# New order constants, TensorE squares for the weights and half chunks in a fused block-sparse attention and MoE kernel

## The chip, the cores and the metric

The kernel runs on one core of a Trainium2 chip. The metric is the device time of one execution in microseconds (us). An execution counts as changed when it differs from the time before by more than 2%.

## The reference

Block-sparse attention over 4 batches, 8 heads, 768 positions and 64 dimensions, followed by a feed-forward layer over the resulting 3072 tokens of width 512. Inputs and outputs are float32, except that the two weight matrices come as 8-byte floats and the sampled blocks as 8-byte integers.

```python
scores = (q @ k.transpose(0, 1, 3, 2)) / sqrt(64)          # 768 x 768 per head
mask = |block_i - block_j| <= 1                            # blocks of 32 positions
mask |= block_i in (0, 23) or block_j in (0, 23)           # first and last block: always
mask |= block_j in sampled_blocks[block_i]                 # 3 random blocks for each row block
attn = softmax(where(mask, scores, -1e9))
x = (attn @ v) as 3072 tokens x 512
h = x @ w_in                                               # w_in 512 x 2048
g = max(h, 0) + alpha * min(h, 0)                          # alpha: one per column of h
return g @ w_out                                           # w_out 2048 x 512
```

## The kernel before

**Precision.** Matmuls run in float16, and float32 accuracy comes from splits: a matrix is scaled by a power of two and split into a high part "hi" (the float16 nearest to it) and a low part "lo" (what is left). A product is then three products: hi by hi, hi by lo, lo by hi. The power of two comes from the sum of the matrix's squares.

**Attention.** A unit is one batch, one tile of 128 queries and one quad of heads: 48 units, of which 8 (the last query tile of each batch) are dense and 40 sparse. A sparse unit has scores against the always present and the neighbouring blocks (tile `sp`, from `kt` with `qt` and `qs`), scores against the random blocks (`sp` from `kr`, which GpSimd gathers with block numbers held in registers), a softmax (VectorE writes `e` and the maximum `nm`, ScalarE the exponential), a split of the probabilities (`ph`), their transpose by DMA (`pt`), and products with the values: random ones (`vr`, gathered by SyncE's DMAs with block numbers in registers), boundary ones (`vb`) and the rest (`v`), all into `av`. Two quads make a tile of x, which is split (`xn`) and transposed by DMA.

**Feed-forward.** 12 chunks of 256 tokens. A chunk has 8 "up" groups and 8 "down" groups. An up group is 24 matmuls 128x256 into the one tile `h` that TensorE has for it (L1174); VectorE then makes `g` of it (L1183 twice, L1184), ScalarE `gh` (L1188), GpSimd `gl` (L1192), and a down group is 12 matmuls 128x512 into the chunk's two `o` tiles (L1209).

**Weights.** 16 pieces of each matrix arrive as raw 8-byte words (512 KB a piece) on the queues of SyncE and ScalarE. VectorE rebuilds float32 from them in three steps (L1033, L1040, L1045), ScalarE sums the squares (L390), and the split follows. w_in has one scale for each pair of pieces. w_out has a single scale: the squares of all 16 pieces are summed (`otot`, a matmul `tot<-ident,otot`, L565) before any piece is split, and so before the first down group. w_in's raw words lie in the space that w_out takes later; w_out's raw words lie in spare buffers of `x` and `vr`.

**Order.** A planner (class Plan) is given every operation with a priority, the engines that may take it, an estimate of its cost and the buffers it needs, and writes out one list for each engine while the program is built. At run time each engine works strictly through its list, and so does each engine's DMA queue: an instruction that waits holds up everything behind it on its engine, DMA issues included. Changing a priority therefore changes what stands behind what.

**Start.** GpSimd loads the sampled blocks by nine DMAs (L276, L281, L286) and clamps them (`sidx`, L315), VectorE packs them in pairs (`spack`), and GpSimd and SyncE load them into registers (L323).

Of the kernel before, what the change touches and what calls it, by code (L numbers as in the profile page):

```python
# [8 lines left out]
F32 = mybir.dt.float32  # L9
# [17 lines left out]
MOE_LAG = 14.222  # L27
MOE_BOOST = 7.439
V_WI = 2.0
W_WI = 0.799  # L30
V_WO = 4.06
W_WO = 1.152
WI_LO = "pe"
PL_W = 30.0
PL_V = -46.0
P_V = -3.693
P_K0, P_K1 = -10.0, 3.746
KB0, KB1, KL0, KL1 = -5.461, -8.133, -22.947, -14.0
VB0, VB1, VL0, VL1 = -4.453, -6.0, -20.0, -9.725
GK, GV = (6, 3), (5, 3)  # L40
P_Q, PL_Q = 10.31, 12.632
A_UP = 0.511
X_UP = 0.863
LD = 3
LAG = 0
# [4 lines left out]
K_PE = 2  # L50
Q_PE = 1
P_PE = 0
# [16 lines left out]
class Plan:  # L69
# [5 lines left out]
    LAT = {"PE": 0.2, "DVE": 0.2, "ACT": 0.2, "POOL": 0.15}  # L75
# [26 lines left out]
    def run(self):  # L102
# [46 lines left out]
        while left:  # L149
            progress = True  # L150
            while progress:
# [4 lines left out]
                for o in ready:  # L156
                    if not self.fits(o.alloc):
                        continue
                    best = min(o.alts, key=lambda e: max(idle[e] - now, hold(o, e)) + load[e] + cost(o, e))
# [57 lines left out]
def attn_moe(ctx: ExitStack, tc: tile.TileContext, q, k, v, sampled, w_in, w_out, alpha, out):  # L217
# [53 lines left out]
    smp = sampled.bitcast(I32).rearrange("a (r w) -> a r w", w=2)  # L271
    srow = cpool.tile([P, NT, NR, 2], I32, name="srow")
    for g in range(NG4):
        rows = [4 * t + 1 + g for t in range(TS)]
        part = srow[g * BLK : (g + 1) * BLK]
        nc.gpsimd.dma_start(  # L276
            part[:, :TS].rearrange("p t r w -> p t (r w)"),
            smp[rows[0] : rows[-1] + 1 : 4].rearrange("t r w -> t (r w)").partition_broadcast(BLK),
        )
        last = (4 * TS + 1 + g) % NBLK  # L280
        nc.gpsimd.dma_start(  # L281
            part[:, TS].rearrange("p r w -> p (r w)"),
            smp[last].rearrange("r w -> (r w)").partition_broadcast(BLK),
        )
    rawp = cpool.tile([P, NBLK * NR * 2], I32, name="rawp")
    nc.gpsimd.dma_start(rawp[BLK : BLK + 1], smp.rearrange("a r w -> (a r w)").unsqueeze(0))  # L286
    sraw = rawp[BLK : BLK + 1].rearrange("p (a r w) -> p a r w", r=NR, w=2)
    al_r = rawp[:NF, :P].bitcast(F32)
    nc.gpsimd.dma_start(al_r, alpha.rearrange("(f p) -> f p", p=P))
# [5 lines left out]
    spare = wi[:, 0, : 2 * P].bitcast(U8)  # L295
# [4 lines left out]
    for x in phs:  # L300
# [12 lines left out]
    ident16 = cpool.tile([P, P], F16, name="ident16")  # L313
    nident = cpool.tile([P, P], F16, name="nident")
    nc.gpsimd.tensor_scalar(sidx, sraw[:, :, :, 0], 0, NBLK - 1, ALU.max, ALU.min)  # L315
    pairs = sidx.rearrange("p a r -> p (a r)")[:, NR : NR + TS * NG4 * NR].rearrange("p (n w) -> p n w", w=2)
    nc.vector.scalar_tensor_tensor(
        spack, pairs[:, :, 1], 16, pairs[:, :, 0], ALU.logical_shift_left, ALU.bitwise_or
    )
    idx = {}  # L320
    for name, eng in (("g", nc.gpsimd), ("s", nc.sync)):
        regs = [eng.alloc_register(name=f"{name}{i}") for i in range(TS * NG4 * NR // 2)]
        eng.load(regs, spack)  # L323
        idx[eng] = []
        for r in regs:
            v = eng.snap(r)
            idx[eng] += [
                nc.s_assert_within(x, 0, NBLK - 1, skip_runtime_bounds_check_because="clamped to this range before the load")
                for x in (v & 0xFFFF, v >> 16)
            ]  # L330
    nc.gpsimd.tensor_copy(sf, srow[:, :, :, 0])
# [16 lines left out]
    nc.gpsimd.tensor_copy(ident16, ident)  # L348
# [60 lines left out]
    LQ3 = {"ACT": 1.3, "SP": 1.0}  # L409
    MAX4 = {"DVE": (0.57, 0), "ACT": 0.89, "POOL": 1.05}  # L410
# [463 lines left out]
    def gather(u, gate):  # L874
        b, t, c = units[u]
        n = 4 * u
        T["krb", u] = plan.buf("kr")
        T["okr", u] = plan.op(n - 4, {"POOL": 3.2}, lambda: emit_kr(u), o_kt[b, c] + chain("kr"), [T["krb", u]], [kbuf[b, c]])
        tail["kr"] = T["okr", u]
        if c == 0:  # L880
            T["vrb", b, t] = plan.buf("vr")
            T["ovr", b, t] = plan.op(n - 3, {"SP": 6.3}, lambda: emit_vr(b, t), o_scr[b] + gate + chain("vr"), [T["vrb", b, t]], dma=2.0)
# [120 lines left out]
    isum = cpool.tile([P, NF], F32, name="isum")  # L1003
    osum = cpool.tile([P, NF], F32, name="osum")
# [7 lines left out]
    def emit_load_w(e, name, f, h):  # L1012
        if name == "wi":
            r = wo.rearrange("p a b -> p (a b)").bitcast(I32)[:, (f % 8) * 1024 : (f % 8 + 1) * 1024]
            load(e, r.rearrange("p (c j) -> p c j", j=W2), wi_src[:, f, :, :])
            T["raw", name, f, h] = r
            return
        t = wt(h.pool, [P, 1024], I32, "raw")
        load(e, t, wo_src[:, f, :])
        T["raw", name, f, 0] = t  # L1020
# [26 lines left out]
    def emit_w_sq(name, f):  # L1047
        w, acc = (wi, isum) if name == "wi" else (wo, osum)
        squares(w[:, f + 1, :], acc[:, f : f + 1])

    def emit_g_norm(g):
        T["itot", g] = ps_h.tile([P, W2], F32, tag="h", name="itot")
        for i in range(2):
            nc.tensor.matmul(T["itot", g][:, 0:1], ones, isum[:, 2 * g + i : 2 * g + i + 1], start=(i == 0), stop=(i == 1))
# [25 lines left out]

    def wparts(name, f):
        w, w16 = (wi, wi16) if name == "wi" else (wo, wo16)
        s = ssc[:, f // 2 : f // 2 + 1] if name == "wi" else s_wo
        return w[:, f + 1, :], w16[:, f, 512:1024], w16[:, f + 1, 0:512], s
# [9 lines left out]
    def emit_sid(g):  # L1094
        T["sid", g] = wt("sid", [P, P], F32)
        nc.gpsimd.tensor_scalar(T["sid", g], ident, ssc[:, g : g + 1], 1.0, ALU.mult, ALU.mult)

    def emit_w_lo_pe(f):
        w, hi, lo, s = wparts("wi", f)
        T["d", f] = ps_o.tile([P, 512], F32, tag="o", name="d")  # L1100
        nc.tensor.matmul(T["d", f], T["sid", f // 2], w, start=True, stop=False)  # L1101
        nc.tensor.matmul(T["d", f], nident, hi, start=False, stop=True)

    def emit_w_lo_copy(f):
        w, hi, lo, s = wparts("wi", f)
        nc.scalar.copy(lo, T["d", f])

    def win(hl, f, c):
        o = 512 if hl == 0 else 0
        return wi16[:, f + hl, o + c * P : o + (c + 1) * P]  # L1110

    def wout(hl, f):
        o = 512 if hl == 0 else 0
        return wo16[:, f + hl, o : o + 512]
# [5 lines left out]
    o_wi, o_wo, o_n3 = {}, {}, {}  # L1120
    n3wi, sqs, gs = {}, {}, []
    for f in range(NF):
        p = V_WI + W_WI * f
        o = plan.op(p - PL_W, LQ, lambda e, f=f: emit_load_w(e, "wi", f, 0), [n3wi[f - 8]] if f >= 8 else [], [plan.buf("ld")], dma=1.6)
        o = plan.op(p, {"DVE": (0.4, 0)}, lambda f=f: emit_n1("wi", f, 0), [o])
        o = plan.op(p, {"ACT": 1.27, "DVE": (0.65, 0)}, lambda e, f=f: emit_n2(e, "wi", f, 0), [o])
        n3wi[f] = plan.op(p, {"DVE": (0.65, 0)}, lambda f=f: emit_n3("wi", f, 0), [o])
        sqs[f] = plan.op(p, {"ACT": 0.8}, lambda f=f: emit_w_sq("wi", f), [n3wi[f]])
        if f % 2 == 1:
            hb = plan.buf("h")  # L1130
            o = plan.op(p - 2, {"PE": 0.8}, lambda g=f // 2: emit_g_norm(g), [sqs[f - 1], sqs[f]], [hb])
            gs.append(plan.op(p - 2, {"DVE": 0.27}, lambda g=f // 2: emit_g_scale(g), [o], [], [hb]))
            prev = o_wi.get(f - 2)
            sb = plan.buf("sid")
            o_sid = plan.op(p, {"POOL": 0.5}, lambda g=f // 2: emit_sid(g), [gs[-1], prev], [sb])
            for x in (f - 1, f):
                o = plan.op(p + 0.1, {"ACT": 0.63, "DVE": (0.36, 0), "POOL": 0.82}, lambda e, x=x: emit_w_hi(e, "wi", x), [gs[-1], prev])
                if WI_LO == "pe":
                    db = plan.buf("o")
                    o = plan.op(p - 2, {"PE": 1.2}, lambda x=x: emit_w_lo_pe(x), [o, o_sid], [db], [sb])  # L1140
                    prev = o_wi[x] = plan.op(p, {"ACT": 0.5}, lambda x=x: emit_w_lo_copy(x), [o], [], [db])
                else:
# [202 lines left out]
```

## Time and profile before

| | |
|---|---|
| median of 3 runs | 851.91 us (842.58, 851.91, 854.73) |
| profiled execution | 850.29 us, its span 848.5 us |
| mean granted TensorE clock | 0.935 |
| busy TensorE / VectorE / ScalarE / GpSimd | 724.1 / 610.0 / 381.9 / 353.2 us |
| DMA | 137.95 MB, mean 163 GB/s |

The span starts with the first instruction and ends with the last; the profiled execution is 1.8 us longer than its span. In the views shown further down, a row of the timeline has the start and duration in us, engine, line, operation, tiles, and in brackets the idle time before it and what ended it. A row of groups has a count, then busy us and mean ns of one, then the idle time before. A row of the table by stage has the stage, its length, then busy us (and instructions) of TensorE matmuls, TensorE weight loads, VectorE, ScalarE and GpSimd, then the granted clock, the DMA engines' busy share and GB/s. A share of the DMA engines can read a little over 1.

### The profile page before, as it was taken

What the parts mean: (1) busy time and instruction counts of PE and PEld (TensorE: products, weight loads), DVE (VectorE), ACT (ScalarE), POOL (GpSimd) and SP (SyncE); (2) the same over time, 40 slices, a digit from 0 to 9 for tenths busy, and PEclk for the clock granted to TensorE, in tenths of its full rate; (3) what the DMA queues carried; (4) which work ended last, traced back from release to release, by engine and by line L of the source; (5) the groups of instructions that cost most, each with busy time, mean ns of one, the idle gap of its engine ahead of it and who ended that gap; (6) DMA issues with size and microseconds to landing.
All of it is one profiled execution on the core that took longest, in us unless ns stands there. A gap on an engine that the chain in (4) does not pass through costs nothing.

```text
span 848.5 us, 24338 instructions
## 1 busy us (share of the span) xinstructions
PE 724.1 (85%) x9163; PEld 502.7 (59%) x9163; DVE 610.0 (72%) x1444; ACT 381.9 (45%) x846; POOL 353.2 (42%) x670
## 2 busy tenths in 40 slices
PE   0644834779998799799999989899999999999997
PEld 0522523556676477566776666576767676667664
DVE  1796679889998576669987747787886677776332
ACT  2654544647544342546644415544444444443111
POOL 4582326534528332735374625321545343121221
PEclk9956865799999899999999999999999999999999
DMA  7799599999999798998977989999776989464000
GB/s 146 212 268 240 143 179 226 210 197 172 188 171 174 187 175 147 195 182 159 208 153 158 193 158 184 181 186 171 136 169 170 178 161 187 76 127 76 23 16 25
DMA packets 359094, 137.95 MB, mean 163 GB/s; under 512 B 326320, under 2 KB 340672, under 8 KB 358976
## 3 DMA queue, kind: packets, MB, share of 16 engines
q1 hardware_dynamic: 304416, 107.92, 67.1%
q10 hardware_dynamic: 54240, 28.45, 14.2%
q8 instruction: 72, 1.18, 0.6%
q14 instruction: 46, 0.38, 0.2%
q0 software_dynamic: 320, 0.03, 0.1%
HBM read 56.65 MB, written 12.58 MB: 82 GB/s over the span
## 4 chain that ended last, share of the span: by engine, by line
PE 56%; DVE 15%; DMA 12%; issue 7%; POOL 4%; ACT 3%; SPq 1%; POOLq 1%; ACTq 1%; DVEq 0%
PE o L1209 21%; PE h L1174 21%; PE sp L638 6%; PE av L638 5%; DMA pt<-ph 3%; DVE ph L402 3%; DVE g L1183 2%; DMA raw<-in_moe_w_out_dram 2%; DMA vr<-scr 1%; PE d L1101 1%; POOL kr L633 1%; POOL gl L1192 1%; DMA qf<-in_q_dram 1%; DVE e L722 1%; DVE wo L402 1%
## 5 line engine op out<-in xcount | busy, mean ns | idle before, releaser
L1174 PE MATMUL h<-x,wi 128*128 128x256 f16 x2304 | 270.8, 275 | 14.9 <-DVE g L1184 13.6
L1192 POOL TENSOR_TENSOR gl<-g,gh 128x512 f16<-128x512 f32 x96 | 120.8, 1259 | 318.4 <-ACT gh L1188 289.9
L1174 PEld LDWEIGHTS <-wi 128*128 128x128 f16 x2304 | 223.7, 99 | 49.8 <-issue 16.6
L1209 PE MATMUL o<-wo,gh 128*128 128x512 f16 x768 | 233.5, 386 | 6.1 <-ACT gh L1188 6.1
L633 POOL COPY kr<-kt 128x128 f16 x480 | 162.1, 388 | 61.0 <-PE sp L638 56.0
L1188 ACT CAST gh<-g 128x512 f16<-128x512 f32 x96 | 59.1, 615 | 216.1 <-DVE g L1184 168.1
L1209 PE MATMUL o<-wo,gl 128*128 128x512 f16 x384 | 147.8, 385 | 6.2 <-POOL gl L1192 6.2
L1183 DVE TENSOR_SCALAR g<-h,am 128x256 f32<-128x256 f32 x192 | 83.7, 477 | 89.2 <-PE h L1174 78.2
L402 DVE SCALAR_TENSOR_TENSOR ph<-e,ph 128x704 f16<-128x704 f32 (+1 forms) x110 | 109.6, 1004 | 14.2 <-ACT ph L394 13.8
L1209 PEld LDWEIGHTS <-gh 128*128 128x128 f16 x768 | 71.4, 99 | 80.1 <-ACT gh L1188 7.1
L729 ACT ACTIVATE e<-e,nm 128x352 f32<-128x352 f32 x160 | 92.6, 579 | 48.6 <-DVE nm L722 28.0
L722 DVE CUSTOM_DVE_ANT_0 e<-sp,bias,cs 128x352 f32<-128x352 f32 x160 | 87.7, 576 | 10.4 <-PE sp L638 10.4
L638 PE MATMUL sp<-kt,qt 128*128 128x192 f16 (+2 forms) x384 | 66.2, 246 | 25.8 <-DVE nm L722 24.6
L638 PEld LDWEIGHTS <-pt 96*32 96x32 f16 (+1 forms) x3456 | 74.0, 99 | 21.7 <-issue 8.5
L638 PEld LDWEIGHTS <-qt 128*32 128x32 f16 (+1 forms) x1024 | 47.6, 101 | 51.2 <-issue 29.3
L1184 DVE SCALAR_TENSOR_TENSOR g<-h,gsc,g 128x512 f32<-128x512 f32 x96 | 72.1, 751 | 3.4
L1209 PEld LDWEIGHTS <-gl 128*128 128x128 f16 x384 | 38.1, 99 | 57.0 <-POOL gl L1192 11.0
L638 PE MATMUL sp<-kt,qs 128*128 128x192 f16 (+2 forms) x384 | 66.2, 246 | 0.5 <-DVE vtot L570 0.5
L394 ACT ACTIVATE ph<-e 128x704 f16<-128x704 f32 (+1 forms) x68 | 54.4, 803 | 3.1 <-DVE g L1183 1.8
L638 PE MATMUL av<-v,pt 128*128 128x64 f16 x1056 | 55.2, 195 | 0.0
L638 PEld LDWEIGHTS <-qs 128*32 128x32 f16 (+1 forms) x1024 | 43.6, 102 | 5.2 <-issue 2.3
L747 ACT ACTIVATE e<-e,nm 128x768 f32<-128x768 f32 x32 | 29.8, 933 | 37.1 <-DVE nm L743 29.5
(153 smaller groups left out, 781.6 us busy)
## 6 DMA issues: line engine op xcount, KB each, us to landing
vr<-scr SPq DMA_DIRECT2D x240, 64.0 KB, 2.6
wo<-in_moe_w_in_dram SPq DMA_DIRECT2D x12, 512.0 KB, 4.7
raw<-in_moe_w_out_dram SPq DMA_DIRECT2D x12, 512.0 KB, 4.8
qs<-qt SPq DMA_DIRECT2D x46, 128.0 KB, 3.5
out_dram<-ob ACTq DMA_DIRECT2D x20, 256.0 KB, 4.0
scr<-v SPq DMA_DIRECT2D x10, 384.0 KB, 3.2
kf<-in_k_dram ACTq DMA_DIRECT2D x9, 384.0 KB, 5.4
vf<-in_v_dram ACTq DMA_DIRECT2D x24, 128.0 KB, 5.7
```

The source lines that it names most:

```text
L394: nc.scalar.activation(dst, src, AF.Copy, scale=scale)
L402: nc.vector.scalar_tensor_tensor(dst, src, scale, hi, ALU.mult, ALU.subtract)
L633: nc.gpsimd.tensor_copy(kr[:, :, g, r * BLK : (r + 1) * BLK], kt[:, :, bass.ds(i * BLK, BLK)])
L638: nc.tensor.matmul(dst, lhs, rhs, start=start, stop=False, skip_group_check=True)
L722: nc.vector.tensor_tensor_reduce(T["e", u, h // 2][:, h % 2, :CS], T["sp", u, h][:, :CS], bias[:, t], scale=T["cs", b, t][:, c : c + 1], s ...
L729: nc.scalar.activation(e, e, AF.Exp, bias=T["nm", u, h], scale=-1.0, accum_out=su_of(u, h))
L1174: nc.tensor.matmul(ph[:, i, :], win(w, f, ct), x[:, l, ct, :], start=(m == 0), stop=(m == len(terms) - 1))
L1183: nc.vector.tensor_scalar(g[:, i, :], ph[:, i, :], 0.0, am1[:, f : f + 1], ALU.min, ALU.mult)
L1184: nc.vector.scalar_tensor_tensor(g, ph, gsc[:, j : j + 1], g, ALU.mult, ALU.add)
L1188: nc.scalar.copy(T["gh", c, j], T["g", c, j])
L1192: nc.gpsimd.tensor_tensor(T["gl", c, j], T["g", c, j], T["gh", c, j], ALU.subtract)
L1209: nc.tensor.matmul(T["o", c][t], g[:, i, t * P : (t + 1) * P], wout(w, f), start=(f == 0 and m == 0), stop=(f == NF - 1 and m == 2),)
```

## The change

Eleven edits, in one step.

1. The priorities and planner constants are new numbers. A penalty (PEN0, PEN1) is added to VectorE's cost wherever the planner chooses between engines, so more splits go to GpSimd and ScalarE. LD (weight loads under way at once) goes from 3 to 2.
2. Weight loads are issued by ScalarE alone (W_ACT), `vb` loads by SyncE alone.
3. The sampled blocks come by one DMA to all partitions, and the register loads become operations of the plan.
4. The weights' squares are summed on TensorE: a pair of pieces is 8 matmuls 128x128 of a block with itself (bf16, the high half of each float32; tile `wsq`), and VectorE takes the diagonal of each. 16 pairs in all.
5. ScalarE's other squares (q, k, v) are written to `rawp` instead of a part of `wi`.
6. The chain of splits of each matrix, in which a piece waited for the piece before it, is cut in two halves that run beside each other.
7. Any of three engines may make `sid` (the scaled identity by which TensorE makes w_in's low part).
8. w_out is taken in reverse; 9 of its 16 pieces wait in w_out's own space (SLOT), 7 in the buffers of `x` and `vr`.
9. `emit_act`: two instructions 128x256 become one of 128x512 with a broadcast factor.
10. The first two chunks run in halves of 128 tokens: 4 up groups of 48 matmuls 128x128 and 4 down groups of 12 matmuls 128x512 for each half.
11. Q_PE goes from 1 to 3 and P_PE from 0 to 2: the first query tiles and the first units' probabilities are transposed on TensorE instead of by DMA.

```diff
-MOE_LAG = 14.222
+MOE_LAG = 13.556
...
-V_WO = 4.06
-W_WO = 1.152
+V_WO = -2.805
+W_WO = 1.818
...
-LD = 3
+LD = 2
+PEN0, PEN1 = 0.3, 0.72
+W_ACT = 1
+HALF = 2
+Q_PE = 3
+P_PE = 2
...
-    smp = sampled.bitcast(I32).rearrange("a (r w) -> a r w", w=2)
...
+    smp = sampled.bitcast(I32).rearrange("a (r w) -> (a r w)", w=2)
+    rawp = cpool.tile([P, 3 * W2 // 4], I32, name="rawp")
+    nc.gpsimd.dma_start(rawp[:, : NBLK * NR * 2], smp.partition_broadcast(P))
...
+    o_regs = {
+        "POOL": plan.op(-11, {"POOL": 3.5}, lambda: emit_regs(nc.gpsimd, "g"), [o_pack]),
+        "SP": plan.op(P_REG, {"SP": 3.5}, lambda: emit_regs(nc.sync, "s"), [o_pack]),
+    }
...
-            o_vb[b, t] = plan.op(n - 3, LQ3, lambda e: emit_vb(e, b, t), o_scr[b] + gate, [vbb[b, t]], dma=0.6)
+            o_vb[b, t] = plan.op(n - 3, {"SP": 1.0}, lambda e: emit_vb(e, b, t), o_scr[b] + gate, [vbb[b, t]], dma=0.6)
...
+    SLOT = {15: 0, 14: 1, 12: 2, 11: 3, 9: 0, 8: 1, 6: 2, 5: 1, 4: 0}
...
-    def emit_w_sq(name, f):
-        w, acc = (wi, isum) if name == "wi" else (wo, osum)
-        squares(w[:, f + 1, :], acc[:, f : f + 1])
+    def emit_w_sq(name, fs, tag):
+        w = wi if name == "wi" else wo
+        t = T["wsq", name, fs[0] // 2] = (ps_h if tag == "h" else ps_o).tile([P, 512], F32, tag=tag, name="wsq")
+        blocks = [
+            w[:, f + 1, c * P : (c + 1) * P].bitcast(BF16).rearrange("p (e w) -> p e w", w=2)[:, :, 1]
+            for f in fs for c in range(NC)
+        ]
+        for i, x in enumerate(blocks):
+            nc.tensor.matmul(t[:, :P], x, x, start=(i == 0), stop=(i == len(blocks) - 1))
...
-        for i in range(2):
-            f = 2 * j + i
-            nc.vector.tensor_scalar(g[:, i, :], ph[:, i, :], 0.0, am1[:, f : f + 1], ALU.min, ALU.mult)
-        nc.vector.scalar_tensor_tensor(g, ph, gsc[:, j : j + 1], g, ALU.mult, ALU.add)
+        a2 = am1[:, n * j : n * j + n].unsqueeze(2).broadcast_to([P, n, w])
+        nc.vector.scalar_tensor_tensor(g, ph, 0.0, a2, ALU.min, ALU.mult)
+        for i in range(0, n, 2):
+            f = (n * j + i) // 2
+            nc.vector.scalar_tensor_tensor(g[:, i : i + 2], ph[:, i : i + 2], gsc[:, f : f + 1], g[:, i : i + 2], ALU.mult, ALU.add)
...
+    for half in range(2):
+        prev = None
+        for f in range(half * NF // 2, (half + 1) * NF // 2):
+            prev, o_wo[f] = split("wo", f, p + 0.1 * f, [o_swo], prev, f < W_PE, o_sid, sb)
...
+    def whole(c):
+        if c >= HALF:
+            return moe(c)
+        for half in range(2):
+            moe(c, half)
```

The lists of the engines show what moved. At the start of SyncE's list, before (`kf`, `qf`, `vf` are raw keys, queries and values of the first batch; `wo<-in_moe_w_in_dram` is a raw piece of w_in):

```order
L323 TENSOR_LOAD spack
L326 ISA x3
L418 DMA kf<-in_k_dram 128x12x64
L418 DMA qf<-in_q_dram 128x8x64
L418 DMA kf<-in_k_dram 128x12x64
L418 DMA vf<-in_v_dram 128x4x64 x3
L418 DMA wo<-in_moe_w_in_dram 128x4x256 x2
```

and in the changed kernel:

```order
L425 DMA kf<-in_k_dram 128x12x64
L425 DMA qf<-in_q_dram 128x8x64
L425 DMA kf<-in_k_dram 128x12x64
L425 DMA vf<-in_v_dram 128x4x64 x3
L368 TENSOR_LOAD spack
L371 ISA x3
L425 DMA vf<-in_v_dram 128x4x64 x6
```

The register load now stands behind the first keys, queries and values, and the raw pieces of w_in have left this list.

The last two raw pieces of w_out, before, on SyncE's list (`x<-xn`, `pt<-ph` and `qt<-qn` are transposes by DMA; `kf` and `qf` here belong to the second batch):

```order
L793 DMA_TRANSPOSE x<-xn 128x8x128
L772 DMA_TRANSPOSE pt<-ph_102 128x12x128
L418 DMA raw<-in_moe_w_out_dram 128x1024
L465 DMA_TRANSPOSE qt<-qn 128x8x128
L418 DMA kf<-in_k_dram 128x12x64 x2
L418 DMA qf<-in_q_dram 96x8x64
L418 DMA qf<-in_q_dram 32x8x64
L418 DMA raw<-in_moe_w_out_dram 128x1024
L772 DMA_TRANSPOSE pt<-ph_103 128x12x128
```

and the last one in the changed kernel, on ScalarE's list (`e,su<-e,nm` is the exponential of a pair of heads, `gh<-g` the feed-forward's high part):

```order
L1249 CAST gh<-g 128x512
L736 ACTIVATE e,su<-e,nm 128x352
L400 ACTIVATE ph_95<-e 128x2x352
L425 DMA raw<-in_moe_w_out_dram 128x1024
L1249 CAST gh<-g 128x512
L736 ACTIVATE e,su<-e,nm 128x352 x2
L789 CAST xn<-xf 128x512
L1049 ACTIVATE raw<-raw 128x512
L425 DMA kf<-in_k_dram 128x12x64 x2
```

The last piece has changed queues, and the second batch's keys now follow it instead of standing ahead of it; ahead of it stand softmax and feed-forward instructions of ScalarE.

On TensorE the matmul `tot<-ident,otot` has, before, ahead of it the scores of units 1 to 8, the random scores of units 1 to 8 and five up groups; in the changed kernel the scores and random scores of units 1 to 7 and the work of four up groups (four half groups of 48 matmuls). The first down group comes behind it in both, and by the scores of unit 11 both lists have issued 13 up and 12 down groups. From there on the two lists stay level to the end.

More of the change, by code (lines that the diff above doesn't have):

```diff
@@ L158, in run @@
                         continue
-                    best = min(o.alts, key=lambda e: max(idle[e] - now, hold(o, e)) + load[e] + cost(o, e))
+                    best = min(o.alts, key=lambda e: max(idle[e] - now, hold(o, e)) + load[e] + cost(o, e) + (PEN0 if now < 150 else PEN1) * (e == "DVE"))
                     if hold(o, best) > 1e-9:
@@ L269, in attn_moe @@
     v_nat = [v[b].rearrange("h (t p) d -> p t h d", p=P) for b in range(B)]
-    smp = sampled.bitcast(I32).rearrange("a (r w) -> a r w", w=2)
[L272 to L289, printed above, removed]
+    smp = sampled.bitcast(I32).rearrange("a (r w) -> (a r w)", w=2)
+    rawp = cpool.tile([P, 3 * W2 // 4], I32, name="rawp")
+    nc.gpsimd.dma_start(rawp[:, : NBLK * NR * 2], smp.partition_broadcast(P))
+    sraw = rawp[:, : NBLK * NR * 2].rearrange("p (a r w) -> p a r w", r=NR, w=2)
+    ident16 = cpool.tile([P, P], F16, name="ident16")
+    nc.gpsimd.tensor_copy(ident16, ident)
     wi = cpool.tile([P, NF + 1, 512], F32, name="wi")
@@ L1122, in attn_moe @@
+    prev = None
     for f in range(NF):
         p = V_WI + W_WI * f
[L1124 to L1128, printed above, removed]
+        slots[f % 8].append(weights("wi", f, p, p - PL_W, None, slots[f % 8][-1:], []))
@@ new lines, in attn_moe @@
+    o_gsc = plan.op(V_WI + W_WI * NF - 2, {"DVE": 0.5}, emit_gsc, gs + [o_al])
+    osq, done = [], {}
+    for n, f in enumerate(reversed(range(NF))):
+        p = V_WO + W_WO * n
+        s, rb = SLOT.get(f), None
+        if s is None:
+            rb = plan.buf(*RAWP)
+        deps = slots[s][-1:] if s is not None else [slots[3][-1]]
+        o = weights("wo", f, p, p - PL_O, rb, deps, slots[(f + 1) // 2][-1:])
+        done[f] = o
+        if s is not None:
+            slots[s].append(o)
+        if f % 2 == 0:
+            osq.append(norms("wo", f // 2, p, [done[f], done[f + 1]]))
@@ L1194, in emit_fs, with emit_gh, emit_gl @@
+    def emit_gh(c, j, half):
+        g = T["g", c, j, half]
+        T["gh", c, j, half] = wt("gh", list(g.shape), F16)
+        nc.scalar.copy(T["gh", c, j, half], g)
+    def emit_gl(c, j, half):
+        g = T["g", c, j, half]
+        T["gl", c, j, half] = wt("gl", list(g.shape), F16)
+        nc.gpsimd.tensor_tensor(T["gl", c, j, half], g, T["gh", c, j, half], ALU.subtract)
     def emit_fs(b):
@@ L1290, in attn_moe @@
                     late.append(u)
-                    uv = late.pop(0) if len(late) > LAG and LAG else None
+                    uv = None
                     o = random_part(u, uv)
```

323 lines of the change are left out of this document (180 added, 143 removed).

## The prediction

> **What bounds the kernel now.** I read the page first: the engines' shares, the slices, and the chain of work that ended last.
>
> ```profile
> span 848.5 us, 24338 instructions
> PE   0644834779998799799999989899999999999997
> PEclk9956865799999899999999999999999999999999
> DMA  7799599999999798998977989999776989464000
> PE 56%; DVE 15%; DMA 12%; issue 7%; POOL 4%; ACT 3%; SPq 1%; POOLq 1%; ACTq 1%; DVEq 0%
> ```
>
> A slice is 21 us. TensorE is nearly full from the ninth slice on and half empty in the first eight, where the DMA engines are the full ones. So there are two kernels here, and I cut the time where the empty part ends: at `tot<-ident,otot`, the matmul that releases w_out's scale and with it every down group.
>
> ```profile
> 177.04 0.49 PE L565 MATMUL tot<-ident,otot 128*128 128x128 f32 x2
> 0.00:177.00 177.00, 89.38 (x1077) 60.99 (x1077) 126.38 (x314) 90.39 (x216) 85.30 (x183) 0.76 0.94 204
> 177.00:245.00 68.00, 63.96 (x829) 43.38 (x816) 63.42 (x150) 39.81 (x77) 31.13 (x31) 0.97 0.89 171
> 245.00:845.00 600.00, 570.72 (x7274) 398.35 (x7271) 420.24 (x982) 251.65 (x553) 236.73 (x457) 0.98 0.78 150
> ```
>
> Before 177 us TensorE is busy 89.4 us and idle 87.6, with the DMA engines at 0.94. Behind it TensorE is busy 634.7 of 668 us at a clock of 0.97 to 0.98. The waits of the last stage are small ones:
>
> ```profile
> PE h L1174 <- DVE g L1184: 9.1, 10, 4.1
> PE o L1209 <- POOL gl L1192: 6.2, 6, 3.4
> PE o L1209 <- ACT gh L1188: 6.1, 3, 3.2
> ```
>
> Hence **the time is that of `tot<-ident,otot`, plus TensorE's work behind it, plus some 30 us of idle**. The change can save much only by making that matmul earlier. What makes it late begins with the start, and ends with the last raw piece of w_out:
>
> ```profile
> 1.54 0.82 POOL L276 DMA_DIRECT2D srow<-in_sampled_blocks_dram  x1 [0.24 <-issue]
> 10.30 0.47 POOL L315 TENSOR_SCALAR sidx<-rawp 1x72 int32<-1x72 int32 x1 [1.50 <-DMA rawp<-in_sampled_blocks_dram]
> 14.03 0.47 SPq L418 DMA_DIRECT2D kf<-in_k_dram  x1
> 21.52 1.01 PE L484 MATMUL tot<-kss,ones 128*128 128x1 f32 x4 [10.12 <-ACT wi L390]
> 71.92 0.59 ACT L1106 CAST wi<-d 128x512 f16<-128x512 f32 x1 [10.10 <-DMA vb<-scr]
> 160.18 0.39 SPq L418 DMA_DIRECT2D raw<-in_moe_w_out_dram  x1
> 174.14 0.69 DVE L1045 SCALAR_TENSOR_TENSOR wo<-raw,wo 128x512 int32<-128x512 int32 x1
> raw<-in_moe_w_out_dram SPq DMA_DIRECT2D x12, 512.0 KB, 4.8
> ```
>
> SyncE's first key load goes out at 14 us, behind the register load. ScalarE stands 10 us at 72 us because `vb` loads that wait for the values stand ahead of a copy of w_in. The last raw piece is issued at 160.2 and lands 4.8 later, at 165; 12 us pass for the three rebuilding steps, squares and sum.
>
> **The change, part by part.** First the transport of the empty stage, which has to move w_in and w_out before `otot`, and half the second batch with it.
>
> ```profile
> q1 hardware_dynamic: 56232, 28.93, 77.3%
> q10 hardware_dynamic: 11024, 6.95, 15.8%
> 0.00:20.00 20.00, 0.26 (x1) 0.18 (x1) 3.07 (x17) 4.01 (x8) 9.79 (x45) 1.00 0.72 141
> 80.00:100.00 20.00, 15.24 (x215) 9.08 (x214) 12.83 (x35) 8.32 (x23) 7.72 (x12) 0.67 0.59 172
> pt<-ph SPq DMA_TRANSPOSE x14, 6.0
> qt<-qn SPq DMA_TRANSPOSE x4, 5.5
> qs<-qt SPq DMA_DIRECT2D x8, 128.0 KB, 5.6
> ```
>
> These rows are of 0 to 177 us, where q10 is ScalarE's queue and q1 SyncE's. ScalarE's has plain loads alone: 0.158 x 177 us for 6.95 MB is 4.02 us of all engines for a MB. SyncE's took 136.8 us. Its transposes are 14 `pt` of 0.39 MB by their shape, 4 `qt` and 2 of x of 0.26 each, 7 MB; the other 22 MB are plain, 88 us at that price, so the 20 transposes cost 48 us together, 2.4 each, an estimate. Q_PE and P_PE take away four of these in this stage (2 `qt`, 2 `pt`), 9.7 us, and four `qs` of 128 KB, 2.1. The second batch's two keys, one query and three values, 1.44 MB or 5.8 us, move behind the last raw piece. Work ahead of the landing was 165 x 0.94 = 155 us, and becomes 155 - 11.8 - 5.8 = 137. The two weak stretches quoted (0.72 and 0.59) belong to the late start and to queues standing behind `vb` and `vr`; the first mends, since with the register load behind them the first keys can go out at about 1 us instead of 14. At 0.97 the landing comes at 142 us; at full use 137, at the old 0.94 146, and if the queue holds the last piece as before, 156 to 165. I take 142, the value next to the busiest stretches, and so **-23 us**, between -28 and 0.
>
> Does something else hold `otot`? VectorE is busy 126 of 177 us; it loses the work moved to GpSimd and gains 16 diagonals, each a 128x128 reduction, below the 0.48 us of a 128x256 row. ScalarE gives up 32 squares:
>
> ```profile
> L390 ACT ACTIVATE wi<-wo 128x512 uint8<-128x512 f32 x16 | 10.0, 626 | 12.7 <-DVE wo L1045 4.8 <-DVE wo L1040 4.0 <-issue 3.5
> 25.20 1.46 PE L522 MATMUL kp<-ident,ph 128*128 128x128 f16 x12 [2.67 <-DVE ph L402]
> ```
>
> That is 10.0 us less, and as much again for w_in's 16, against 32 loads' issues and some `ph` high parts more. TensorE gains 128 matmuls 128x128, which the row of `kp` puts at 0.12 each, 15 us at most, and some 30 to 60 transposes for `qt`, `qs` and `pt`, 4 to 7 more: about 20 us into 87.6 of idle. **0**, and without that cover up to +20. Such an added wait stands on TensorE's strict list: behind a `wsq` whose piece is late the next scores wait, and behind them VectorE and ScalarE.
>
> Behind `otot`, TensorE has one up group, one unit's scores and one unit's values more than before.
>
> ```profile
> 783.12 2.79 PE L1174 MATMUL h<-x,wi 128*128 128x256 f16 x24
> 178.90:183.40 4.50, 1.99 (x46) 0.82 0.50 149
> 176.50:177.10 0.60, 0.60 (x51) 1.00 0.36 92
> 782.60 0.69 PE L638 MATMUL av<-v,pt 128*128 128x64 f16 x18
> ```
>
> The up group is 2.6 us by the start of its successor, the scores (unit 9's, in the second row, at a clock of 0.82) about 1.6 at full clock, the random values 0.5: **+4.7 us**. Half groups have twice the matmuls at half the width. In the last row 18 matmuls of 64 columns, each with its own weight load, take 0.52 us to the next start, 29 ns each; a matmul of 128 columns takes twice a 64-column one or more, so weight loads stay hidden and a half group costs the same 2.6 us: **0**, at worst +3 for the 16 half up groups if the loads show by 4 ns each in 768 matmuls.
>
> The feed-forward's VectorE work:
>
> ```profile
> L1183 DVE TENSOR_SCALAR g<-h,am 128x256 f32<-128x256 f32 x192 | 83.7, 477 | 89.2 <-PE h L1174 78.2
> L1184 DVE SCALAR_TENSOR_TENSOR g<-h,gsc,g 128x512 f32<-128x512 f32 x96 | 72.1, 751 | 3.4
> ```
>
> Now 2 x 0.477 + 0.751 = 1.705 us for a group. With two of the second kind 1.50, 0.2 less for each of 80 whole groups, 16 us of VectorE; half groups (one 0.75, two of 128x256 at 0.48) stay at 1.7. This meets TensorE only in the 9.1 us of waits on `g`, of which I take a fifth: **-2**, between -6 and 0. Registers, `sid` and `rawp` for the other squares cost nothing of their own: ScalarE and GpSimd are busy 90 and 85 us of the first 177, and without that room each would cost its own one to three us once. The choice of queues is in the landing above.
>
> First down groups: a half's four down groups read all 16 pieces of w_out, where before one group read two. VectorE is busy 63.4 of 68 us in that stage, so pieces come at its pace; the two half chains and the pieces given to GpSimd relieve it. I take **+2**, between 0 and +12.
>
> Sum: 850.3 - 23 + 4.7 + 0 - 2 + 2 = **832 us** against the profiled execution's 850.3, which is 1.6 under the median shown; I let the difference stand, as it is below what three runs tell.
>
> **The rivals.** *The head start is all.* The last piece now stands on ScalarE's list behind exponentials and feed-forward copies, and waits there for a staging buffer that TensorE frees, with the feed-forward's next `gh` and exponentials queued behind it; if these queues and not the transport time it, only the gain at the start stays. There the first norm of the keys came at 21.5 and the landing can move by at most the 12 to 13 us of the first load, of which the ten us of ScalarE's squares behind it give some 9: 850.3 - 9 + 4.7 - 2 + 1 = 845. For it: the waits for VectorE and `vb` on the lists. Against it: DMA at 0.94.
>
> *GpSimd becomes late; this is the one that ends slower.* Its list gains 16 pairs that split probabilities and 6 that split keys, 15 low parts of x and some weights.
>
> ```profile
> L405 POOL TENSOR_TENSOR ph<-e,ph 128x704 f16<-128x704 f32 x2 | 3.6, 1814 | 0.2
> L404 POOL TENSOR_SCALAR e<-e 128x704 f32<-128x704 f32 x2 | 2.3, 1141 | 1.5 <-ACT ph L394 0.8 <-DVE rs L751 0.6
> L1192 POOL TENSOR_TENSOR gl<-g,gh 128x512 f16<-128x512 f32 x96 | 120.8, 1259 | 318.4 <-ACT gh L1188 289.9 <-issue 15.2 <-PE o L1209 9.9
> L1192 POOL TENSOR_TENSOR gl<-g,gh x96: 1149/1157/1863, 160.9 to 840.6; 128x512 f16<-128x512 f32 x96
> L1188 ACT CAST gh<-g 128x512 f16<-128x512 f32 x96 | 59.1, 615 | 216.1 <-DVE g L1184 168.1
> ```
>
> A pair is 2.95 us. An up and a down group last 5.2, and `g`, `gh`, `gl` take 1.50 + 0.62 + 1.26 = 3.4, which leaves 1.8: a pair ahead of a `gl` makes the down group 1.2 late, or up to 2.95 where nothing else is in hand. 22 pairs at 2.07 are 46 us, and with a landing 19 earlier 850.3 - 19 + 46 = 877. It decides once more than about nine pairs hit. Against it: three `gl` buffers and a GpSimd idle for 360 of 600 us in the last stage.
>
> The Trainium skill's page "SBUF — State Buffer", section "SBUF: two separate sides", says that VectorE with two SBUF inputs and a GpSimd instruction that reads SBUF share a port pair as an exclusive lock, and that whichever comes second waits for the whole instruction. By that rule more work on GpSimd also slows VectorE. The trace agrees so far that most `gl` take their least time, 1.15 us, and the longest 1.86. What the rule would add here is not above this rival's 46 us, by my estimate, since the lock is held for one instruction at a time.
>
> *First down groups wait for all pieces.* If the splits go at VectorE's old pace, the fourth half group is 12 us late: 843. *Every wait of the first stage goes*, and the landing comes at 125 us: 812.
>
> **How the numbers follow.** Forecast 832 (818 to 842): 0.56. Head start alone, 845: 0.23. First down groups, 843: 0.07. All waits gone, 812: 0.06. GpSimd late, 877: 0.08. The bound of 2% (what a measurement here can tell from no change) lies at 834.9 and 868.9 around the median of 851.9. Some four fifths of the first case and the 812 lie below it: faster 0.51; slower 0.08; same 0.41. The range leaves out the GpSimd case and the far end of the early one: 808 to 853.
>
> **What would show it.** SyncE's first key load at about 1 us and `tot<-kss,ones` near 12; the last raw piece landing near 142 and `tot<-ident,otot` near 154; 0.9 or more in the stretches that had 0.72 and 0.59; TensorE's waits on `gl` at some 6 us as now; some 676 us from `otot` to the end, where now it is 671. It is wrong if `otot` comes before 140 or after 163, or if waits on `gl`, `gh` or `g` exceed 40 us.

## The result: 842.1 us, half of the forecast gain

The changed kernel took a median of 842.10 us (836.94 to 849.41, 20 runs) against 853.09 (20 runs) before: a ratio of 0.990, with a 95% interval of 0.9871 to 0.9929. By the bound of 2% that counts as no change; the interval lies below 1, so a gain of about 1% is clear of the noise. The time is inside the range, but 832 had been forecast, a gain about twice as large. Executions more than 1.5% above the fastest of their kernel are left out of the medians and ratios below, and the traces of three runs (the low parts of keys and probabilities to VectorE, the squares on ScalarE, the early keys in the kernel before) are of such executions. The profiled execution took 839.76 us and its span is 837.9, against 850.29 and 848.5 before.

The page of the changed kernel, its slices and the chain that ended last:

```profile
span 837.9 us, 25406 instructions
PE   1766667769999898989999979899999799999997
PEclk9967769699999999999999999999999999999999
DMA  9868997999898589999967799899968887363100
PE 56%; DMA 12%; SPq 9%; DVE 8%; issue 6%; POOL 5%; ACT 2%; ACTq 1%; POOLq 1%; DVEq 0%
```

TensorE is fuller in the first eight slices. VectorE's share of the chain fell from 15% to 8%, and SyncE's queue (SPq) rose from 1% to 9%: a new cause of waiting. The start and the two ends that the forecast names, in the timeline of the changed kernel:

```profile
0.73 0.46 SPq L425 DMA_DIRECT2D kf<-in_k_dram  x1
9.41 0.47 POOL L330 TENSOR_SCALAR sidx<-rawp 1x72 int32<-1x72 int32 x1
15.58 1.01 PE L491 MATMUL tot<-kss,ones 128*128 128x1 f32 x4 [5.39 <-ACT rawp L396]
137.74 0.34 ACTq L425 DMA_DIRECT2D raw<-in_moe_w_out_dram  x1
157.23 0.78 PE L572 MATMUL tot<-ident,otot 128*128 128x128 f32 x2
```

The first keys go out at 0.73 us, the last raw piece of w_out at 137.7 instead of 160.2 (it lands at 143.1), and w_out's scale comes 19.8 us earlier. The two stages on each side of it, first of the kernel before, then of the changed one (columns as in the table by stage shown before):

```profile
0.00:177.00 177.00, 89.38 (x1077) 60.99 (x1077) 126.38 (x314) 90.39 (x216) 85.30 (x183) 0.76 0.94 204
177.00:848.50 671.50, 634.68 (x8100) 441.73 (x8086) 483.66 (x1131) 291.46 (x630) 267.86 (x487) 0.98 0.79 152
```

```profile
0.00:157.00 157.00, 96.02 (x1252) 69.32 (x1253) 117.08 (x313) 84.72 (x160) 76.99 (x175) 0.78 0.91 209
157.00:837.90 680.90, 639.34 (x8480) 453.15 (x8480) 432.01 (x998) 319.89 (x673) 340.86 (x563) 0.98 0.78 152
```

Ahead of the scale TensorE is busy 6.6 us more and idle 26.6 us less (61.0 instead of 87.6). Behind it TensorE is busy 4.7 us more and idle 4.7 us more (41.6 instead of 36.8). Those two give back 9.4 of the 20 us. The idle time rises right behind the scale: from 4.0 to 8.6 us in the first 68 us, from 32.8 to 33.0 in the rest. What TensorE waits for behind the scale, before and then changed (in total, times, longest):

```profile
PE h L1174 <- DVE g L1184: 9.1, 10, 4.1
PE o L1209 <- POOL gl L1192: 6.2, 6, 3.4
PE o L1209 <- ACT gh L1188: 6.1, 3, 3.2
PE av L638 <- DMA pt<-ph: 2.9, 2, 2.4
```

```profile
PE av L645 <- DMA pt<-ph: 18.7, 6, 5.1
PE h L1231 <- DVE g L1244: 13.6, 7, 3.9
PE o L1275 <- POOL gl L1254: 0.8, 2, 0.6
```

Of the waits on `g`, 7.7 us now fall in the first 68 us behind the scale, where there were none. In the rest, the waits on `gl` and `gh` have all but gone, but 15.8 us of waits on `pt`, the transposed probabilities, have come. At the second longest of them SyncE's queue shows why:

```profile
472.44 2.26 SPq L425 DMA_DIRECT2D vb<-scr  x3
474.80 1.30 SPq L779 DMA_TRANSPOSE pt<-ph  x1
476.38 7.50 SPq L630 DMA_DIRECT2D vr<-scr  x12
483.98 1.23 SPq L800 DMA_TRANSPOSE x<-xn  x1
485.26 1.22 SPq L425 DMA_DIRECT2D qs<-qt  x2
486.53 6.83 SPq L779 DMA_TRANSPOSE pt<-ph  x3
```

SyncE issues without a pause, and the transpose that TensorE waits for until 492.6 stands behind a gather of 7.5 us and three of the `vb` loads that edit 2 gave to this queue.

### The profile page after: what moved, and what is told of

It reads as the page before. It is cut to its first block, busy times and chain, and to the rows that moved or that the text cites. A ratio compares the mean times of both kernels' runs of the same rounds, so it can differ in the third digit from the quotient of the medians.

```text
span 837.9 us, 25406 instructions
## 1 busy us (share of the span) xinstructions
PE 735.4 (88%) x9731; PEld 522.5 (62%) x9731; DVE 549.1 (66%) x1311; ACT 404.6 (48%) x832; POOL 417.9 (50%) x738
## 4 chain that ended last, share of the span: by engine, by line
PE 56%; DMA 12%; SPq 9%; DVE 8%; issue 6%; POOL 5%; ACT 2%; ACTq 1%; POOLq 1%; DVEq 0%
PE h L1231 22%; PE o L1275 21%; PE av L645 6%; PE sp L645 5%; SPq L630 5%; DMA pt<-ph 3%; DMA vr<-scr 3%; SPq L425 2%; POOL kr L640 1%; DVE ph L408 1%; DVE e L729 1%; DMA raw<-in_moe_w_out_dram 1%; SPq L779 1%; POOL gl L1254 1%; DVE g L1244 1%
## 5 line engine op out<-in xcount | busy, mean ns | idle before, releaser
L1231 PE MATMUL h<-x,wi 128*128 128x256 f16 (+1 forms) x2688 | 278.0, 263 | 15.6 <-DVE g L1244 14.4
L1231 PEld LDWEIGHTS <-wi 128*128 128x128 f16 x2688 | 234.8, 101 | 45.9 <-DVE g L1244 15.8
L1275 PE MATMUL o<-wo,gh 128*128 128x512 f16 x768 | 228.6, 379 | 0.0
L640 POOL COPY kr<-kt 128x128 f16 x480 | 152.2, 367 | 55.5 <-PE sp L645 46.3
L1241 DVE SCALAR_TENSOR_TENSOR g<-h,am 128x512 f32<-128x512 f32 x96 | 66.2, 689 | 122.7 <-PE h L1231 117.0
L1275 PE MATMUL o<-wo,gl 128*128 128x512 f16 x384 | 145.6, 379 | 0.9 <-POOL gl L1254 0.8
L408 DVE SCALAR_TENSOR_TENSOR ph<-e,ph 128x704 f16<-128x704 f32 (+1 forms) x94 | 94.4, 1007 | 25.9 <-ACT ph L400 25.6
L400 ACT ACTIVATE ph<-e 128x704 f16<-128x704 f32 (+1 forms) x92 | 73.7, 804 | 33.4 <-DMA pt<-ph 22.1
L1244 DVE SCALAR_TENSOR_TENSOR g<-h,gsc,g 128x512 f32<-128x512 f32 (+1 forms) x112 | 74.1, 674 | 3.4
L743 DVE CUSTOM_DVE_ANT_0 e<-sp,dbias,cs 128x384 f32<-128x384 f32 x64 | 38.9, 613 | 19.6 <-PE sp L645 18.6
```

The lines of the kernel that those rows point to most:

```text
L400: nc.scalar.activation(dst, src, AF.Copy, scale=scale)
L408: nc.vector.scalar_tensor_tensor(dst, src, scale, hi, ALU.mult, ALU.subtract)
L640: nc.gpsimd.tensor_copy(kr[:, :, g, r * BLK : (r + 1) * BLK], kt[:, :, bass.ds(i * BLK, BLK)])
L1231: nc.tensor.matmul(ph[:, i, :], win(k, f, ct), x[:, l, ct, cols], start=(m == 0), stop=(m == len(terms) - 1))
L1241: nc.vector.scalar_tensor_tensor(g, ph, 0.0, a2, ALU.min, ALU.mult)
L1244: nc.vector.scalar_tensor_tensor(g[:, i : i + 2], ph[:, i : i + 2], gsc[:, f : f + 1], g[:, i : i + 2], ALU.mult, ALU.add)
```

## The experiments

Each kernel is the changed kernel with one edit unless it says otherwise. Where an edit only gives an operation to another engine, the order written out by the planner is kept. Ratios are to the kernel before, with 95% intervals; the changed kernel has 0.990 (0.9871 to 0.9929).

**What holds the stage behind w_out's scale?** From the scale to the start of the fourth down group pass 38 us (24 in the kernel before), and GpSimd is busy for 31.8 of them. Three runs gave part of its work to VectorE, a fourth took the halves away.

```diff
+        prev.tag = name + "_lo"
...
     for o in plan.run():
+        if getattr(o, "tag", "") in ('wo_lo',) and o.eng == "POOL":
+            o.eng = "DVE"
```

> The changed kernel with one edit: the five low parts of w_out that GpSimd makes go to VectorE, at the same places of the order. Theory G (behind w_out's scale GpSimd's strict list holds back the feed-forward's low parts gl, and with them g's buffers and TensorE): the pieces take 5 x 2.7 us out of GpSimd's list between 160 and 185 us, the gl that ran at 181.5 comes some 10 us sooner, the fourth down group ends at about 187 instead of 194.9, and the whole takes 834 (833 to 837). Theory S (the half chunks wait for all 16 split pieces, which VectorE's pace sets): VectorE gains 4.6 us of work there, the down groups come no sooner, 842 to 846.

843.32 us, ratio 0.9853 (0.9807 to 0.9899).

```diff
...
     for o in plan.run():
+        if getattr(o, "tag", "") in ('k_lo', 'p_lo') and o.eng == "POOL" and o_swo.start <= o.start < o_swo.start + 40:
+            o.eng = "DVE"
```

> The changed kernel with one edit: the four low parts of keys and probabilities that GpSimd makes in the stage right behind w_out's scale go to VectorE, at the same places of the order. Theory G: 4 x 2.3 to 3.2 us leave GpSimd's list there, the late gl comes 4 to 8 us sooner, the whole takes 836 to 839. Theory S: nothing that the pieces of w_out wait for changes, but VectorE gets 4 us more: 842 to 845.

841.66 us, 0.9842 (0.979 to 0.9894).

Both edits together:

> The changed kernel with the edits of the two runs before it together: five low parts of w_out and four of keys and probabilities from GpSimd to VectorE. Theory G: no more than the first alone brings, about 834, since GpSimd is no longer late and VectorE, at 63 of 81 us busy in that stage, gets 8.5 us more; TensorE's waits on VectorE's g grow. Theory S: 846 or more.

843.68 us, 0.987 (0.9824 to 0.9916). None of the three differs from the changed kernel beyond the intervals. In the first and third the fourth down group starts at 195 us, as without the edit. In the third, with GpSimd relieved, VectorE's rows follow one another without a gap from 167 to 186 us, and the group that feeds the second down group again comes at the end of them:

```profile
182.41 1.16 POOL L1257 TENSOR_TENSOR gl<-g,gh 128x512 f16<-128x512 f32 x1 [6.75 <-ACT gh L1252]
186.35 2.85 PE L1234 MATMUL h<-x,wi 128*128 128x128 f16 x48 [1.82 <-DVE g L1247]
```

Taking work from GpSimd does not bring the down groups sooner, so theory G falls. VectorE is then busy for 58.8 of the first 68 us behind the scale instead of 52.6. That the work of splitting, wherever it is done, sets the pace there fits, but no run took it from both engines.

```diff
-HALF = 2
+HALF = 0
```

> The changed kernel with HALF = 0: all chunks run whole, as before the change. The planner writes the lists anew. Theory S: the first down group again needs two pieces of w_out instead of four, and 834 to 838 results. Theory G: the half chunks are not what costs; GpSimd's list holds the same low parts, 840 to 847, and the first gl behind w_out's scale is late again.

848.71 us, 0.9932 (0.9899 to 0.9964): at or above the changed kernel, not below. Theory S's time fails as well. Since the lists were written anew, and TensorE waits for `gh` (10.1 us) and `gl` (6.1) again, the run does not price the half chunks alone. What a half group costs stands in the traces. A whole group of the kernel before, with the row behind it:

```profile
263.46 2.79 PE L1174 MATMUL h<-x,wi 128*128 128x256 f16 x24
266.08 0.69 PE L638 MATMUL av<-v,pt 128*128 128x64 f16 x18
```

and two half groups of the changed kernel:

```profile
224.57 2.84 PE L1231 MATMUL h<-x,wi 128*128 128x128 f16 x48
227.25 0.69 PE L645 MATMUL av<-v,pt 128*128 128x64 f16 x18
184.79 4.48 PE L1231 MATMUL h<-x,wi 128*128 128x128 f16 x48 [3.85 <-DVE g L1244]
189.11 0.59 PE L1275 MATMUL o<-wo,gh 128*128 128x512 f16 x2
```

At a granted clock of 1.00 the half group takes 2.68 us from its start to the next row's, the whole one 2.62: 0.06 more, 1 us for all 16. The last one takes 4.32 us at a granted clock of 0.60, right behind a wait of 3.85 us. Two more of the 16 were slow, 4.95 us at 0.54 and 3.71 at 0.73.

**SyncE's queue.** All `vb` loads back to ScalarE:

```diff
+        if o in o_vb.values():
+            o.eng = "ACT"
```

> The changed kernel with one edit: every vb load is issued by ScalarE instead of SyncE, at the same places of the order. Theory P (in the stage that TensorE fills, what is lost against the forecast is the 20 us in which TensorE waits for pt, because SyncE's list holds vb and the 7.5 us of a vr gather ahead of the transposes): SyncE issues 57 vb loads of about 0.6 us less, the waits on pt fall to some 10 us, the whole takes 834 to 839. Theory Q (SyncE's list is not what times pt, or ScalarE then stands for vb as before the change): 842 or more, with ScalarE waiting on vb's source.

847.06 us, 0.9922 (0.9895 to 0.995). Not faster, but the trace (of its fastest execution, 840.44 us) holds both theories, each in its place. From the scale to the end of the twelfth down group it takes 88 us instead of 83: ScalarE stands in front of a split of w_out while its queue is held for 7.3 us by three `vb` loads,

```profile
ACT wo L400 <- DMA qt<-qn: 7.9, 1, 7.9
```

and late, the waits on `pt` fall as theory P says:

```profile
PE av L645 <- DMA pt<-ph: 7.6, 6, 2.4
```

The other way to get `pt` ahead was to put it there:

```diff
+    for v in [o for o in todo if o in list(T.values()) and o.eng == "SP" and o.alts == {"SP": 6.3}][3:]:
...
+        sp = [k for k in range(i + 1, end) if todo[k].eng == "SP"][:4]
+        last = [k for k in sp if getattr(todo[k], "tag", "") == "pt"][:2]
+        if last:
+            todo.insert(last[-1] + 1, v)
+            todo.pop(i)
```

> The changed kernel with one edit: each vr gather from the fourth on goes behind up to two of the pt transposes that followed it within four places on SyncE's list, and all else stays at its place. Theory P: the waits on pt fall from 20 us to under 8, and the whole takes 830 to 836. Theory Q: transposes that wait for their ph now hold the gathers, the waits move to vr, and it takes 842 to 850.

858.25 us, 1.0069 (1.0038 to 1.0101): slower than the kernel before, by 0.7%. TensorE now waits on `vr` for 13.2 us and on `pt` for 18.7 still: turning the order round leaves the one wait and adds another. If the queue simply has too much in it, something must leave it. So the next run takes `vb` away only where the queue is short of time:

```diff
+        if any(o is x and key[0] > 0 for key, x in o_vb.items()):
+            o.eng = "ACT"
```

> The changed kernel with one edit: from the second batch on, vb loads are issued by ScalarE, and the first batch's stay with SyncE. If the run with all of them on ScalarE lost early (tot<-ident,otot to D12, 5 us longer) what it won late (6 us from there to the end), this one keeps the win alone: the waits on pt in the full stage fall from 18.7 to about 8 us and the whole takes 834 to 838. If the late win belongs to something that the early edit did, or ScalarE's gh then come late, it takes 841 to 845.

835.46 us, 0.9796 (0.975 to 0.9842): clearly below the changed kernel. Behind the scale, TensorE's waits are now

```profile
PE h L1231 <- DVE g L1244: 17.6, 9, 3.9
PE av L645 <- DMA pt<-ph: 6.3, 4, 2.6
```

That the later `vb` loads on SyncE's queue cost time is shown. In the trace (of the fastest execution, 831.33 us) 12.4 us of waits on `pt` are gone and 4 more on `g` have come; behind the scale TensorE is idle 38.1 us instead of 41.6 and busy 636.2 instead of 639.3. So a wait that goes is not time won in full, and how the 6.6 us of the median divide is not shown.

**What made the scale earlier?** The place of the scale scatters from trace to trace: four runs above whose edits act only behind it (the first, the third, `pt` ahead of `vr`, later `vb`) have it at 158.46, 159.59, 157.14 and 155.21 us, against 157.23. The forecast said that the transport sets it. The test of that adds transfers that nobody reads:

```diff
+            if f in (2, 5, 8, 11):
+                extra = dram.tile([P, 1024], I32, name=f"extra{f}")
+                load(e, extra.rearrange("p (c j) -> p c j", j=W2), wi_src[:, f, :, :])
```

> The changed kernel with four more transfers of 512 KB on ScalarE's queue beside w_in's pieces 2, 5, 8 and 11, into scratch that nobody reads: 2 MB, 8 us of all DMA engines at the price of the row used in the prediction. Theory D (transport sets the empty stage): tot<-ident,otot comes 6 to 8 us later and the whole takes 848 to 851. Theory L (the engines' strict lists set it, and the DMA engines, at 0.66 to 0.84 between 40 and 80 us, have room): it comes 0 to 3 us later, 842 to 845.

840.89 us, 0.9843 (0.9801 to 0.9885). The DMA engines' share rises from 0.91 to 0.95 and the scale moves by 0.4 us:

```profile
0.00:157.00 157.00, 91.89 (x1251) 67.64 (x1251) 116.74 (x312) 84.22 (x160) 77.49 (x175) 0.81 0.95 223
157.62 0.77 PE L572 MATMUL tot<-ident,otot 128*128 128x128 f32 x2
```

Theory D falls: a share of 0.9 had room for 2 MB. The four transfers were issued between 16 and 40 us, though. In the changed kernel the DMA engines' share is 0.99 from 80 to 120 us, and no run adds to that stretch.

```diff
+    todo = plan.run()
+    todo.remove(o_regs["SP"])
+    todo.insert(todo.index(o_pack) + 1, o_regs["SP"])
+    first = todo.index(o_pack)
+    head = [o for o in todo[:first] if o.eng == "SP"]
+    todo = [o for o in todo[:first] if o.eng != "SP"] + todo[first : first + 2] + head + todo[first + 2 :]
```

> The changed kernel with one edit undone: SyncE loads its registers ahead of its first keys, so the keys go out at about 10 us instead of 0.7. Theory H (the head start is what made w_out's scale, tot<-ident,otot, 20 us earlier): it comes 8 to 11 us later, at 165 to 168, and the whole takes 849 to 853. Theory D (the transport made it, with 12 us less of DMA work and 6 us moved behind): it comes 2 to 5 us later, and the whole takes 844 to 847.

848.09 us, 0.9921 (0.9894 to 0.9949). The first keys go out at 11.35 us, and the scale comes at 162.90, 5.7 us later. For the whole, the median is 6 us up, but the intervals of the ratios overlap.

```diff
...
-            nc.tensor.matmul(t[:, :P], x, x, start=(i == 0), stop=(i == len(blocks) - 1))
+        acc = isum if name == "wi" else osum
+        for f in fs:
+            squares(w[:, f + 1, :], acc[:, f : f + 1])
...
```

> The changed kernel with one edit undone: the weights' 32 sums of squares are made by ScalarE again (26 us with the reads of the sum), at the places where TensorE made them, without wsq and its 14 us on TensorE and without VectorE's diagonals. If ScalarE's list held w_out's scale before the change, it comes 5 to 10 us later and the whole takes 847 to 852; if the 14 us of TensorE are what counts, it takes 830 to 838; if both are covered, as forecast, 842 (840 to 845).

850.58 us, 0.9944 (0.9912 to 0.9976): the median is 8.5 us up, by the ratios it is less, and their intervals overlap a little. Where the scale falls is not read from this run.

```diff
     for o in plan.run():
+        if getattr(o, "tag", "") == "sid":
+            o.eng = "POOL"
```

> The changed kernel with one edit undone: all eight scaled identities sid are made by GpSimd again, at the same places of the order. If the 11 us by which TensorE's waits for sid shrank (14.5 before, 3.6 after) are what the squares and the start leave unexplained of the 19.8 us of tot<-ident,otot (10.6 and 5.6 when each was undone), it comes 3 to 6 us later and the whole takes 845 to 849. If those waits lay beside others, it comes 0 to 1 us later, 842.

837.03 us, 0.9802 (0.976 to 0.9844): neither theory, but faster than the changed kernel. TensorE's waits on `sid` grow from 3.6 to 10.1 us, and still the scale comes at 154.21, 3 us sooner and a little beyond the scatter: these waits lay beside others. ScalarE's list is the shorter for it (busy 82.5 us ahead of the scale instead of 84.7), but that this made the gain is not shown.

Squares on ScalarE, registers first and `sid` on GpSimd together:

> The changed kernel with three edits undone together: squares on ScalarE, registers ahead of the first keys, sid on GpSimd. If the three times add, tot<-ident,otot comes 16 to 21 us later, at 173 to 178, about where it was before the change, and the whole takes 857 to 863. If they hide behind one another, it comes 10 to 13 us later and the whole takes 850 to 855, and the other edits of the first stage carry the rest.

853.37 us, 0.9989 (0.9954 to 1.0025): clearly above the changed kernel and at the time of the kernel before, since the changed kernel's longer stretch behind the scale stays. The scale is at 167.02, 10 us later than in the changed kernel and 10 earlier than in the kernel before. Ahead of it, TensorE's waits on `nm` go back to 17.3 us (19.2 before, 7.1 changed) and those on `sid` to 14.6 (14.5 and 3.6). The three do not add up to 19.8; other edits carry the rest, and they were not taken apart.

The head start alone, in the kernel before:

```diff
-    for name, eng in (("g", nc.gpsimd), ("s", nc.sync)):
+    def load_regs(name, eng):
...
+    load_regs("g", nc.gpsimd)
...
     def picks(eng, t, use):
+        if eng not in idx:
+            load_regs("s", eng)
```

> The kernel before with one part of the change: SyncE loads its registers just ahead of their first use, so its first keys go out at about 1 us instead of 14. By what undoing the same thing in the changed kernel cost (5.6 us of tot<-ident,otot, 6 us of the whole), 846 to 849 against 853.6. If the head start is worth all of the nine us that the forecast's rival gave it, 843 to 845. If the transport or the lists behind it take it back, 851 to 854.

859.48 us, 1.0063 (1.0032 to 1.0094): slower, by 0.6%. The keys go out at 0.74 us, but the nine small loads of the sampled blocks, which had only ScalarE's first loads beside them, now have six of SyncE's as well and land later: the first eight 7.4 us after their issue (median) instead of 4.3, the ninth 6.5 instead of 3.0. Of this trace only the start is read:

```profile
15.73 0.47 POOL L315 TENSOR_SCALAR sidx<-rawp 1x72 int32<-1x72 int32 x1 [5.00 <-DMA rawp<-in_sampled_blocks_dram]
26.98 1.01 PE L485 MATMUL tot<-kss,ones 128*128 128x1 f32 x4 [10.83 <-ACT wi L391]
```

`sidx` comes 5.4 us later, and with it the bias, which stands on ScalarE's list ahead of the second key square; so the first norm of the keys comes 5.5 later, not sooner. In the changed kernel one load brings the blocks, `sidx` is at 9.41 and the norm at 15.58.

**VectorE's fused step, undone:**

```diff
-        nc.vector.scalar_tensor_tensor(g, ph, 0.0, a2, ALU.min, ALU.mult)
+        for i in range(n):
+            nc.vector.tensor_scalar(g[:, i, :], ph[:, i, :], 0.0, am1[:, n * j + i : n * j + i + 1], ALU.min, ALU.mult)
```

> The changed kernel with one edit undone: g's first step is again one instruction of 128x256 (or 128x128 in half chunks) for each piece instead of one of 128x512, at the same places. The forecast's term gives 2 us: 843 to 845, with TensorE's waits on g some 3 us longer. If VectorE's relief is what took away the waits on g, gl and gh of before (21 us then, 7 now), they come back in good part: 848 to 856.

844.84 us, 0.9878 (0.9832 to 0.9925); the median is 2.7 us up, not beyond the intervals, and the waits on `g` behind the scale go from 13.6 to 17.6. The term of 2 us is not contradicted.

**The two that were faster, together** (later `vb` on ScalarE, `sid` on GpSimd):

> The changed kernel with the two edits that each made it faster: vb from the second batch on issued by ScalarE, and sid made by GpSimd alone. One acts behind the first batch, the other ahead of w_out's scale, so their 6.6 and 5.1 us should add: 829 to 833. If sid's gain lay in what the late stage then loses, 835 to 837.

831.62 us, 0.9742 (0.9699 to 0.9786): 10.5 us below the changed kernel in the median, near the sum of 6.6 and 5.1. This is the lowest median of all, though its interval overlaps those of the two. That it is also the 832 of the forecast is chance: the forecast was for the kernel without these two edits.

## Why the gain came out at about half

Against the profiled execution the forecast was -18.3 us, and -10.5 was measured. Of the difference, 3.2 us lie in the place of the scale and 4.7 in idle time behind it.

- **Where the time comes from** held: the place of `tot<-ident,otot` plus TensorE's work behind it plus some idle describes both traces.
- **-23 for the scale**: measured -19.8, inside its bounds, but the size was near by luck. The last piece landed at 143.1 us, where 142 had been forecast, by two errors that cancel: up to then the DMA engines' share was 0.86, not 0.97, and so their work 123 us (143.1 x 0.86), not 137. The first 20 us filled as said (1.02), but from 40 to 60 us the share was 0.66. The step that divided the work by 0.97 took a busy share for a limit. Two more MB moved the scale by 0.4 us, while undoing the squares, the register order and `sid` together moved it by 10 and took the whole gain. The squares had been priced at 0, as covered by ScalarE's idle time. ScalarE was busy half of that stage, but each square stood in a chain (rebuild, square, sum, scale, split) on a strict list; a share of busy time does not show that.
- **The head start** at 0.73 us came as said, and the norm came at 15.6 instead of 12. Given to the kernel before alone, it delayed the small loads of the sampled blocks, and the norm with them; the changed kernel has a single load in their place.
- **+4.7 of TensorE work behind the scale** was measured as +4.7, in part by luck. The `h` matmuls are busy 9.6 us more behind the scale, attention 3.2 more, and the down matmuls, of the same number and shapes, 7.5 less, which was not taken apart. (Three quarters of the near scores of unit 8 still run ahead of the scale, so "one unit's scores" was a little too much.) "Half groups cost the same" held to 1 us, though a matmul of 128 columns took 56 ns, a little less than twice the 29 of 64 columns. Of `h`'s 9.6 us, one more group is 2.8, the width of the half groups 0.7, and two half groups at granted clocks of 0.73 and 0.60 are 2.7.
- **-2 and +2 of waits behind the scale** is the step that failed: together 0 was forecast, and idle rose by 4.7. In the first 68 us it rose by 4.5, inside the bounds of the term for the first down groups (+2, between 0 and +12). In the rest it rose by 0.2 instead of falling by 2. There the relief was far larger than written, 14.7 us of waits on `g`, `gl` and `gh` gone, but 15.8 us on `pt` came, which no term held: "the choice of queues is in the landing above" priced the `vb` loads up to the scale only, and 57 loads moved to SyncE over the whole program. Taking back the later ones gave 6.6 us.
- **Rivals.** "GpSimd becomes late" did not happen as a time: waits on `gl` fell to 0.8 us, and three runs that relieved GpSimd gained nothing shown. "First down groups wait for all pieces", at 843, was nearest in time, and its wait is in the trace: the fourth down group starts 38 us behind the scale instead of 24. But TensorE had other work meanwhile, so its idle time rose by 4.5 us there and not by 12, and whole chunks were not faster. "The head start is all", at 845, was near by the wrong road: undoing the register order moved the scale by 5.7 of the 19.8 us.

What stays open: which of the remaining edits brought the other 10 us of the scale, whether the transfers hold the stretch from 80 to 120 us, and where the gain from `sid` on GpSimd comes from.

## What to carry to other kernels

Price a move from one queue to another over the whole program, stage by stage: it can win where one list is full and lose where the other is, and here the kernel with the lowest median leaves the first batch's `vb` loads on SyncE's queue and gives the later ones to ScalarE. On strictly ordered lists, a half idle engine can still be the limit through the chain it stands in, and a busy share of 0.9 on the DMA engines is not a limit until something added to it moves the end. When transfers start sooner, ask which small ones they will then run beside. And a sum of busy time mixes the cost of an instruction with the clock it was granted: compare single groups, from start to start, at the same granted clock.

## What the runs showed of the hardware

Issuing a gather of twelve 64 KB pieces with addresses from registers held SyncE's queue for 6.5 to 9.8 us in the 17 gathers behind the scale of the changed kernel. One of the `pt` transposes that stand behind them took 1.3 to 4.4 us to issue, half of them at most 1.5.

Eight small loads on GpSimd's queue, of 0.8 and 3.8 KB, landed 7.4 us after their issue (median) instead of 4.3 when SyncE's first keys, query and values started beside them, and the user of the ninth came 5.4 us later. One load of the same blocks to all partitions, beside such traffic in the changed kernel, was used at 9.4 us.

Behind a wait of 3.85 us TensorE's next 48 matmuls ran at a granted clock of 0.60 and took 4.32 us; behind waits of 1.21 and 2.23 us such a group ran at 1.00 and took 2.69.
